# Short products on the identity added at eight places of a fixed order table

## The chip, the cores and the metric

The kernel runs on one core of one Trainium2 chip. The metric is the device time of one execution in microseconds, the median of several runs. The core has a matrix engine (TensorE, PE in the rows), a vector engine (VectorE, DVE), a scalar engine (ScalarE, ACT), a general engine (GpSimd, POOL) and a sync engine that issues transfers (SyncE, SP). They run side by side, each in the order of its own instructions, and wait for each other by semaphores. TensorE writes its results into PSUM, a small memory of eight banks.

## The reference, cut to what matters

A gated linear attention over 4 batches, 8 heads and 768 steps is followed by two feed-forward layers on 3072 rows of 384.

```python
for t in range(S):                                   # attention, D = 48
    state = alpha[:, :, t, :, None] * state + np.einsum('bhd,bhe->bhde', k[:, :, t], v[:, :, t])
    y[:, :, t] = np.einsum('bhd,bhde->bhe', q[:, :, t], state)
...
h = x @ w_in                                         # first layer, d_ff = 2048
g = (a[0] + a[1]*h + a[2]*h**2 + a[3]*h**3) / (1 + |b[0]|*|h| + |b[1]|*h**2 + 1e-6)
x = g @ w_out
...
g = x @ w_gate                                       # second layer, d_ff = 1536
out = (g * (1 / (1 + np.exp(-g))) * (x @ w_val)) @ w_out
```

## The kernel before, in words

The attention is cut into 24 blocks of 128 steps, six to a batch; blocks are numbered from 0 here. For each block TensorE transposes alpha, k and q (`aT`, `kT`, `qT`, each four transposes, line 770), makes the scores (`scores`, line 821), turns k back (`back`, `kn_ps`, line 846) and makes the update of the state and the block's output (`values`, lines 865 to 876: `upd` and `yT`). Between them VectorE scans the decays (`bb`, `cc`) and scales k and q (`kt`, line 802; `qt`, line 812), ScalarE copies results out of PSUM (`al`, `aa`, `kn`, the state `st_s`, and `yo`, line 885, the copy of `yT`), and GpSimd masks the scores and decays the state. SyncE's queue loads the blocks (`nata`, `natk`, `natq`, `natv`, line 729) and stores `yo`. The weights of both layers are loaded and split into a high and a low part (lines 639 to 702, with `win_x` and the like on VectorE, and a PSUM bank of kind `cv`). Each product of the first layer is nine matmuls of 128 x 512 (`mm1` into `h`, `mm2` into three accumulators `acc`, lines 955 to 957); the second layer follows with `pg`, `pv` and `po`. The products of the first layer begin at some 54 us, between the attention blocks.

At the start, nine transposes of the identity (`keep_warm`, line 562) run before there is data, and twenty more behind the first `qT`; they write a PSUM tile called warm.

Every piece of work is an operation of a planner, with a number in the order in which it was planned. Nothing is reordered while the kernel is built: `ORDER` is a written-out table, and each entry holds an operation's number and its way of being done:

```python
for x in table:
    i, k = x >> 1, x & 1
    ...
    yield i, how[k][2]
...
for x, (i, f) in enumerate(plan.order(ORDER)):   # i is an operation's number
```

The eight PSUM banks are given out by `order` as well. An operation that writes a bank first takes the first unit of the list `free`; the unit goes to the end of that list when the table comes to the last operation that uses it, which may be long before that operation has run on the chip. A tile with a bank's tag waits for the readers of that bank's tile before.

Eight operations have a part in the change. For each: the first unit of `free` when the table has come to it, and the operation that the table has as the last reader of that bank before.

| number | operation | what is behind it on TensorE | first free bank, its last reader by the table |
|---|---|---|---|
| 90 | `aT`, block 3 | `values`, block 1 | bank 4: ScalarE, copy of block 1's scores (45) |
| 79 | `values`, block 2 | `scores`, block 3 | bank 7: VectorE, `qt` of block 3 (99) |
| 146 | `aT`, block 5 | `values`, block 3 | no free bank |
| 135 | `values`, block 4 | `scores`, block 5 | bank 2: VectorE, `kt` of block 5 (153) |
| 161 | `values`, block 5 | `kT`, block 7 | bank 5: VectorE, `kt` of block 6 (175) |
| 185 | `values`, block 6 | `scores`, block 7 | bank 3: ScalarE, copy of block 6's scores (181) |
| 281 | `kT`, block 10 | the first `mm2` | bank 6: VectorE, `win_x`, a weight (711) |
| 942 | the first `mm2` | the second `mm2` | bank 2: ScalarE, `yo` of block 8 (241) |

Of the kernel before, what the change touches and what calls it, by code (L numbers as in the profile page):

```python
# [9 lines left out]
F32 = mybir.dt.float32  # L10
# [216 lines left out]
class Plan:  # L227
# [47 lines left out]

    def order(self, table):

        free = {c: list(range(k)) for c, k in self.classes.items()}
        todo = {}
        done = set()  # L280
        for x in table:
            i, k = x >> 1, x & 1
            _, how, deps, writes, follows = self.ops[i]
            assert i not in done and done.issuperset(deps) and done.issuperset(follows)
            done.add(i)
            for b in writes:
                if b.kind and b.ops[0] == i:
                    b.unit = free[b.cls].pop(0)
                    for j in set(b.ops):
                        todo.setdefault(j, []).append(b)  # L290
                    b.open = len(set(b.ops))
            for b in todo.get(i, ()):
                b.open -= 1
                if not b.open:
                    free[b.cls].append(b.unit)
            yield i, how[k][2]
        assert len(done) == len(self.ops)
# [160 lines left out]
def gla_moe_moe2_kernel(  # L458
# [15 lines left out]
    nc = tc.nc  # L474
# [23 lines left out]
    plan = Plan()  # L498
# [5 lines left out]
    ps = main.enter_context(tc.tile_pool(name="ps", bufs=1, space=PSUM))  # L504
# [31 lines left out]
    def fixed(t):  # L536
        b = plan.buf(None)
        b.t = t
        return b
# [10 lines left out]
    ident = const.tile([128, 128], F32, name="ident")  # L550
# [18 lines left out]
    for nm in "akqv":  # L569
        for i in range(NBV if nm == "v" else 1):  # L570
            t = A.tile([128, H, 64], F32, name=f"nat{nm}{i}")
# [164 lines left out]

    FILL = 20
    fixed_warm = fixed(warm)
    params = fixed(prm)

    def load_params():
# [590 lines left out]
    t, vs2 = end_a + 5.14, []  # L1332
# [10 lines left out]
        moe2(row, n, f0, f1, load_y(row[0], n), wg, wv, wo)  # L1343
    flag = bounds(end_a + 70.0, vs2[-1][0] - 70.0, vs2[-1][0] + 20.0)

    for x, (i, f) in enumerate(plan.order(ORDER)):
        if x == len(ORDER) - 18:
            tc.mark_branch_hint_location(
                "usual", "LikelyTaken", [mybir.EngineType.PE, mybir.EngineType.DVE, mybir.EngineType.SP])
        for b in plan.ops[i][3]:  # L1350
            if b.t is None:
                b.t = b.make()
        f()
# [40 lines left out]
```

## Time and profile before

| | us |
|---|---|
| median of 3 runs | 988.63 (988.26 to 989.31) |
| the profiled execution, its time | 987.1 |
| the profiled execution, its span from first to last instruction | 985.3 |

The trace was taken from one execution, so durations and starts are those of that one. A row of a timeline names the start in us, the length in us, the engine, the line, the operation, what is written and read, and how many alike were merged; a bracket holds the engine's idle time before it and what seems to have ended it. Matmuls overlap, so the spacing of starts tells their cost better than their lengths, and the ends of matmuls are modelled. Of a wait for several semaphores only the one that came last by the profile is named.

### The profile page before, as it was taken

The page shows a single profiled execution, that of the slowest core. Times are in us where ns is not written, and L with a number is a line of the kernel's source. Part 1 is how long each engine was busy: PE and PEld are TensorE (multiplying, and loading weights), DVE is VectorE, ACT ScalarE, POOL GpSimd, SP SyncE. Part 2 cuts the span into 40 slices and gives each one's busy share as a digit, 9 for nine tenths or more (in the row PEclk, how much of TensorE's full clock was granted, in tenths as well). Part 3 has the DMA queues.
Part 4 walks back from the last instruction along what each step waited for, and adds up shares of the span by engine and source line. Part 5 has one row for each costly group of instructions (what it writes and reads, how often), then busy time and mean ns, then how long its engine had stood idle before and what let it go on. Part 6 is the DMA issues. An engine that isn't in the chain of part 4 may idle for free.

```text
span 985.3 us, 15291 instructions
## 1 busy us (share of the span) xinstructions
PE 969.0 (98%) x5355; PEld 805.6 (82%) x5355; DVE 786.9 (80%) x1493; ACT 588.9 (60%) x1078; POOL 450.5 (46%) x426
## 2 busy tenths in 40 slices
PE   8899999999999999999999999999999999999997
PEld 7777888888888888888888888888888888888886
DVE  7999999999889888888898896799887767733222
ACT  4588998899999787789988675222122222212111
POOL 3368888799877676777987555000000000000000
PEclk9999999999999999999999999999999999999999
DMA  8978666531223242101221663346665545501000
GB/s 184 208 186 220 150 156 152 157 103 37 57 88 94 54 140 70 55 25 53 91 86 45 218 188 127 113 129 196 176 179 187 165 140 150 161 1 33 1 0 34
DMA packets 167137, 113.51 MB, mean 115 GB/s; under 512 B 115472, under 2 KB 140560, under 8 KB 167056
## 3 DMA queue, kind: packets, MB, share of 16 engines
q1 hardware_dynamic: 166768, 112.10, 40.7%
q8 instruction: 43, 0.70, 0.3%
q10 hardware_dynamic: 288, 0.39, 0.1%
q14 instruction: 38, 0.31, 0.1%
HBM read 95.95 MB, written 16.52 MB: 114 GB/s over the span
## 4 chain that ended last, share of the span: by engine, by line
PE 84%; DVE 8%; ACT 4%; issue 2%; POOL 1%; DMA 1%; SPq 0%; DVEq 0%; ACTq 0%; POOLq 0%
PE acc L955 6%; PE acc L956 6%; PE acc L957 6%; PE h L955 5%; PE h L957 5%; PE h L956 5%; PE pg L957 5%; PE pg L955 5%; PE pg L956 5%; PE pv L957 5%; PE pv L955 5%; PE pv L956 5%; PE po L955 4%; PE po L957 4%; PE po L956 4%
## 5 line engine op out<-in xcount | busy, mean ns | idle before, releaser
L925 POOL TENSOR_TENSOR gg<-t,gg 128x512 fp32r<-128x512 f32 x96 | 129.8, 1352 | 52.2 <-ACT gg L1014 50.9
L998 POOL TENSOR_TENSOR t<-t,t 128x512 f32<-128x512 f32 x96 | 127.7, 1332 | 29.2 <-ACT t L988 20.6
L1177 DVE TENSOR_TENSOR sg<-sg,pv 128x512 f32<-128x512 f32 (+1 forms) x73 | 49.4, 678 | 101.3 <-PE pv L957 101.0
L1179 ACT CAST pp<-sg 128x512 fp32r<-128x512 f32 (+1 forms) x73 | 44.8, 615 | 142.1 <-DVE sg L1177 126.7
L1175 ACT ACTIVATE sg<-pg 128x512 f32<-128x512 f32 (+1 forms) x73 | 43.0, 591 | 144.0 <-PE pg L957 143.8
L955 PE MATMUL h<-xt,win 128*128 128x512 f32 x288 | 114.4, 397 | 0.2 <-DVE wo_x L675 0.2
L955 PE MATMUL acc<-gg,wout 128*128 128x512 f32 x288 | 113.9, 396 | 0.5 <-DVE win_x L675 0.5
L957 PE MATMUL h<-xt,win 128*128 128x512 f32 x288 | 112.4, 390 | 0.0
L957 PE MATMUL acc<-gg,wout 128*128 128x512 f32 x288 | 112.3, 390 | 0.0
L956 PE MATMUL acc<-gg,wout 128*128 128x512 f32 x288 | 112.3, 390 | 0.0
L956 PE MATMUL h<-xt,win 128*128 128x512 f32 x288 | 112.2, 390 | 0.0
L957 PE MATMUL pg<-yy,wg 128*128 128x512 f32 x216 | 84.2, 390 | 0.0
L956 PE MATMUL pg<-yy,wg 128*128 128x512 f32 x216 | 84.2, 390 | 0.0
L955 PE MATMUL pg<-yy,wg 128*128 128x512 f32 x216 | 84.1, 389 | 0.0
L957 PE MATMUL pv<-yy,wv 128*128 128x512 f32 x216 | 84.0, 389 | 0.0
L956 PE MATMUL pv<-yy,wv 128*128 128x512 f32 x216 | 84.0, 389 | 0.0
L955 PE MATMUL pv<-yy,wv 128*128 128x512 f32 x216 | 84.0, 389 | 0.0
L1004 DVE SCALAR_TENSOR_TENSOR t<-t,h 128x512 f32<-128x512 f32 x96 | 65.4, 682 | 19.2 <-ACT h L1003 18.7
L995 ACT ACTIVATE t<-h,prm 128x512 f32<-128x512 f32 x96 | 73.8, 775 | 7.1 <-POOL gg L925 6.7
L1102 DVE TENSOR_SCALAR_CACHE_REDUCE chk_x<-chk_e 128x384 f32<-128x384 uint32 x136 | 73.6, 549 | 2.7
L1002 ACT ACTIVATE t<-t,oneps 128x512 f32<-128x512 f32 x96 | 69.5, 724 | 9.3 <-POOL t L998 8.9
L999 DVE TENSOR_TENSOR t<-t,h 128x512 f32<-128x512 f32 x96 | 65.1, 680 | 10.2 <-ACT t L995 10.0
(154 smaller groups left out, 2472.8 us busy)
## 6 DMA issues: line engine op xcount, KB each, us to landing
chk<-in_moe_w_out_dram SPq DMA_DIRECT2D x28, 384.0 KB, 3.2
yr<-y1d SPq DMA_DIRECT2D x36, 256.0 KB, 2.9
xr<-xd SPq DMA_DIRECT2D x27, 256.0 KB, 3.4
y1d<-ys SPq DMA_DIRECT2D x27, 256.0 KB, 3.2
win_st<-in_moe_w_in_dram SPq DMA_DIRECT2D x16, 384.0 KB, 4.1
wout_st<-in_moe_w_out_dram SPq DMA_DIRECT2D x16, 384.0 KB, 3.9
chk<-in_moe_w_in_dram SPq DMA_DIRECT2D x16, 384.0 KB, 3.5
nata<-in_alpha_dram SPq DMA_DIRECT2D x24, 192.0 KB, 3.6
```

The source lines that it names most:

```text
L925: return lambda: eng.tensor_tensor(out_(), in0(), in1().bitcast(F32), ALU.subtract)
L955: nc.tensor.matmul(out_, wh, xh, start=start, stop=False)
L956: nc.tensor.matmul(out_, wh, xl, start=False, stop=False)
L957: nc.tensor.matmul(out_, wl, xh, start=False, stop=stop)
L995: plan.op(v, [act(T, lambda: nc.scalar.activation(t4(), h(), AF.Identity, scale=a3, bias=a2), 2, False)], (hb,), (b4,))
L998: plan.op(v, [pool(T, lambda: nc.gpsimd.tensor_tensor(t1(), t1(), t2(), ALU.mult))], (b1, b2), (b1,))
L999: plan.op(v, [dve(T, lambda: nc.vector.tensor_tensor(t4(), t4(), h(), ALU.mult))], (b4, hb), (b4,))
L1002: plan.op(v, [act(T, lambda: nc.scalar.activation(t2(), t1(), AF.Ln, bias=oneps), 1)], (b1,), (b2,))
L1004: plan.op(v, [dve(T, lambda: nc.vector.scalar_tensor_tensor(t1(), t1(), ONE_EPS, h(), ALU.add, ALU.mult))], (b1, hb), (b1,))
L1102: [(DVE, 0.5, lambda: nc.vector.tensor_scalar(dst(), src(), bound, 0.0, op_, ALU.add, accum_out=cnt.t[:, c : c + 1]))],
L1177: plan.op(v, [(DVE, 0.07 + 0.53 * d, lambda sg=sg, z=z: nc.vector.tensor_tensor(sg.t[:, z], sg.t[:, z], pv.t[:, z], ALU.mult))], (sg, pv), ...
L1179: plan.op(v, [(ACT, 0.1 + 0.43 * d, lambda sg=sg, pp=pp, z=z: nc.scalar.copy(pp.t[:, 0, z], sg.t[:, z]))], (sg,), (pp,))
```

## The change

A function `fill(n)` is added. It takes the first unit of the planner's list of free banks without removing it, makes a tile in that bank and lets TensorE transpose the identity into it n times; if no bank is free, it does nothing. In the loop over the table it is called right ahead of operation i if i is a key of `fills`, when `order` has already given that operation its own banks. The table itself, and all operations in it, stay as they are. The counts add up to 39.

```diff
     def order(self, table):
 
-        free = {c: list(range(k)) for c, k in self.classes.items()}
+        free = self.free = {c: list(range(k)) for c, k in self.classes.items()}
...
+    def fill(n):
+        x = plan.free["bank"][:1]
+        if x:
+            t = ps.tile([128, 512], F32, tag=f"bank{x[0]}", bufs=1, name="fill")
+            for _ in range(n):
+                nc.tensor.transpose(t[:, 0:128], ident, ident)
...
+    fills = {
+        90: 4, 79: 5, 146: 4, 135: 10, 161: 5, 185: 5, 281: 3, 942: 3,
+    }
     for x, (i, f) in enumerate(plan.order(ORDER)):
+        if i in fills:
+            fill(fills[i])
         if x == len(ORDER) - 18:
```

## Rows read from the trace of the kernel before

**Rows 1.** Cores: span in us and mean granted TensorE clock.
```profile
core 0: 985.3 us, clock 0.998
```

**Rows 2.** Windows: length, busy us of PE, PEld, DVE, ACT, POOL; clock, DMA, GB/s.
```profile
20.00:40.00 20.00, 16.68 (x217) 14.54 (x217) 19.54 (x35) 10.96 (x27) 9.07 (x10) 1.00 0.87 192
37.00:38.00 1.00, 0.00 (x0) 0.00 (x0) 0.89 (x3) 0.93 (x3) 1.00 (x2) 1.00 0.61 182
...
40.00:80.00 40.00, 36.79 (x350) 30.73 (x350) 39.72 (x70) 32.63 (x69) 22.92 (x27) 1.00 0.83 195
80.00:200.00 120.00, 119.52 (x913) 99.57 (x911) 116.82 (x187) 108.69 (x213) 99.03 (x95) 1.00 0.65 167
200.00:979.00 779.00, 778.81 (x3708) 646.40 (x3707) 597.34 (x1188) 427.43 (x754) 313.16 (x276) 1.00 0.33 99
```

**Rows 3.** Timeline of TensorE: its eight waits of over 0.45 us by 100 us.
```profile
17.86 0.62 PE L770 MATMUL aT<-ident,nata 128*112 128x128 f32 x4 [0.63 <-DMA nata<-in_alpha_dram]
...
24.83 0.58 PE L865 MATMUL upd<-natv,kn 128*64 128x48 f32 x15 [0.87 <-ACT st_s L909]
...
30.61 0.62 PE L770 MATMUL aT<-ident,nata 128*112 128x128 f32 x4 [0.70 <-ACT wout L680]
...
38.51 0.58 PE L865 MATMUL upd<-natv,kn 128*64 128x48 f32 x15 [1.61 <-ACT kn L849]
...
44.94 1.31 PE L870 MATMUL yT<-aa,natv 128*64 128x128 f32 x16 [0.82 <-DMA natv<-in_v_dram]
...
51.03 0.58 PE L865 MATMUL upd<-natv,kn 128*64 128x48 f32 x15 [0.78 <-ACT al L779]
...
74.31 0.65 PE L770 MATMUL kT<-ident,natk 128*112 128x128 f32 x4 [0.49 <-DVE st_c L902]
75.49 0.50 PE L955 MATMUL acc<-gg,wout 128*128 128x512 f32 x1 [0.54 <-DVE win_x L675]
```

**Rows 4.** Timeline of TensorE, 6 to 9 us: products on the identity.
```profile
6.08 2.35 PE L562 MATMUL warm<-ident 128*128 128x128 f32 x20
8.26 0.60 PE L770 MATMUL aT<-ident,nata 128*112 128x128 f32 x4
```

**Rows 5.** Timeline of VectorE, 24 to 76 us: some readers of PSUM.
```profile
24.64 0.68 DVE L812 TENSOR_TENSOR qt<-qT,bb 112x512 f32<-112x512 f32 x1
...
30.43 0.68 DVE L802 TENSOR_TENSOR kt<-kT,cc 112x512 f32<-112x512 f32 x1
...
39.38 0.69 DVE L802 TENSOR_TENSOR kt<-kT,cc 112x512 f32<-112x512 f32 x1
...
43.91 0.68 DVE L802 TENSOR_TENSOR kt<-kT,cc 112x512 f32<-112x512 f32 x1
...
50.43 0.68 DVE L812 TENSOR_TENSOR qt<-qT,bb 112x512 f32<-112x512 f32 x1
...
74.91 0.53 DVE L675 SCALAR_TENSOR_TENSOR win_x<-win_st,win_e 128x384 uint32<-128x384 uint32 x1
```

**Rows 6.** Timeline of ScalarE, 28 to 78 us: copies of scores, state and output.
```profile
28.63 0.58 ACT L830 COPY aa<-sc 128x512 f32<-128x512 f32 x1 [3.04 <-PE sc L821]
...
30.93 0.35 ACT L909 COPY st_s<-st_c 48x192 f32<-48x192 f32 x1
...
76.87 0.62 ACT L885 COPY yo<-yT 128x512 f32<-128x512 f32 x1
```

**Rows 7.** Timeline of TensorE, 28 to 50 us: some transposes and one `values`.
```profile
28.87 0.60 PE L770 MATMUL kT<-ident,natk 128*112 128x128 f32 x4
...
31.38 0.58 PE L865 MATMUL upd<-natv,kn 128*64 128x48 f32 x15
...
42.11 0.65 PE L770 MATMUL kT<-ident,natk 128*112 128x128 f32 x4
...
49.21 0.60 PE L770 MATMUL qT<-ident,natq 128*112 128x128 f32 x4
```

**Rows 8.** Timeline of TensorE: its last wait of over 0.2 us.
```profile
141.00 0.61 PE L865 MATMUL upd<-natv,kn 128*64 128x48 f32 x15 [0.41 <-DVE t L1010]
```

## Prediction

> **What bounds the kernel now.** I read the cores first, for the span and the clock, then windows by stage, then TensorE's waits in its timeline, and last VectorE and ScalarE around them. The profiled execution took 987.1 us, 985.3 of them span [rows 1]. The reader is to see two stages. From 200 to 979 us TensorE is busy in 778.81 of 779 us, from 80 to 200 in 119.52 of 120 [rows 2]: what it loses before then comes out at the end. From 20 to 80 us VectorE is busy in 19.54 of 20 and 39.72 of 40 us, and TensorE waits [rows 2, 3]: there VectorE sets the pace, and a delay of VectorE is not made good. The eight waits of the title are all in this part, 6.44 us together [rows 3].
>
> The granted clock is 1.00, the 2.4 GHz level, in each of these windows, also from 37 to 38 us, which holds no matmul at all [rows 2]. There is no slow stretch for the fills to lift.
>
> **What the change adds.** Nothing is removed or moved. The keys are the numbers of the operations that wait, so each fill stands on TensorE right ahead of its wait's operation. The price of a product: twenty begin at 6.08 us, the next transposes at 8.26, so 2.18/20 = 0.109 us [rows 4]. The counts are indeed 0.7 of each wait: 10 x 0.109 = 1.09 of 1.61. At operation 146 the list of free banks is empty, so no fill is made: 35 products, 3.8 us, remain. Were all hidden, they would cost nothing.
>
> But a fill needs a bank, and `free` follows the table, not the chip. A bank stands in it as soon as the table has passed its last reader, and on the chip that reader, on VectorE or ScalarE, may still be waiting for its turn. The fill must wait for it, and the operation behind the fill waits too, though its own bank and data are ready. That is the step on which the time hangs. I take the fills in order.
>
> - Operation 90 (block 3, 4 products, 0.44 us in a wait of 0.63 for a load): the bank was read by ScalarE's copies of block 1's scores, which TensorE has outrun by a full block. Hidden; at most 0.44.
> - Operation 79 (block 2, 5 products): the bank's last reader is VectorE's qt of block 3, 24.64 + 0.68 = 25.32 [rows 5]. `values` itself began at 24.83 [rows 3]. With 0.05 for the signal (as from 75.44, the end of win_x, to the product at 75.49 [rows 3, 5]) and 5 x 0.109, `values` starts at 25.92: 1.09 late. Who waits? The scores of block 3 are behind it on TensorE, ScalarE sat idle 3.04 us for them, and its state copy of block 3, which ends at 30.93 + 0.35 and releases `values` at 31.38 [rows 6, 7], stands behind: 1.1 late again. The load that holds operation 146 takes up part for the transposes alone. On VectorE, kt of block 4 needs transposes that now end at 28.87 + 0.60 + 1.09 = 30.56 [rows 7], and goes from 30.43 to 30.61 [rows 5]: all of VectorE is 0.2 late.
> - Operation 135 (block 4, 10 products): the last reader is kt of block 5, 39.38 + 0.69 + 0.2 = 40.27 [rows 5]. `values` would have begun at 38.51, or some 0.3 later by now [rows 3]. The fill starts at 40.32 and lasts 1.09: `values` at 41.41, 2.9 late. The scores of block 5 and the k transposes behind them move with it, from 42.11 to 45.01, and end at 45.66 [rows 7]; kt of block 6 on VectorE goes from 43.91 to 45.71 [rows 5], 1.8 late.
> - Operation 161 (block 5, 5 products): the bank is read by that kt, until 45.71 + 0.68 = 46.39. Behind the transposes this costs TensorE little; `values` waits for the masks of its late scores anyway. Carry 2.9, less 0.4 if the load named in its row was the last to come [rows 3].
> - Operation 185 (block 6, 5 products, 0.55 in a wait of 0.78): the bank is read by ScalarE's copies of the scores, which are ahead of the masks that `values` needs. Hidden; at most 0.55. TensorE goes on 2.9 late. VectorE's qt at 50.43 needs transposes that end at 49.21 + 0.60 + 2.9 = 52.71 [rows 7]: it starts at 52.76, so VectorE is 2.3 late, and as it is full, so it stays up to 75 us.
> - Operation 281 (block 10, 3 products): the last reader is VectorE's win_x, 74.91 + 0.53 = 75.44 [rows 5], while the transposes began at 74.31 [rows 3]. In the old times: fill at 75.49, out at 75.82, 1.51 late. That win_x also frees the next operation's accumulator, so this alone would matter little.
> - Operation 942 (the first product into the accumulators, 3 products): the last reader is ScalarE's yo of block 8, 76.87 + 0.62 = 77.49 [rows 6], which this product had no need of. Fill at 77.54, product at 77.87 instead of 75.49: 2.38 late. On top of VectorE's 2.3 (ScalarE works off VectorE's results here, so I move yo by the same): 4.7 late at 75 us.
>
> From here TensorE is full and keeps the 4.7. What takes up some of it is the one wait left by 200 us, 0.41 at 141.00 [rows 8]: VectorE and ScalarE are less late than TensorE now, so it goes. The sum: 2.3 + 2.38 - 0.4 = 4.3 us. Profiled execution: 987.1 to 991.4. The median of the runs shown lies 1.5 us above that execution, and on it I forecast 988.63 + 4.3 = **992.9 us**.
>
> Bounds of the uncertain terms: the carry up to 75 us from 0 (if all of it is taken up) to 2.9 (if ScalarE moves with TensorE and not with VectorE); I take 2.3, the row that is nearest. The two fills at 75 us: 2.38, or 2.05 if the three products ran beside other work. The wait at 141: 0 to 0.41 taken up.
>
> Does a waiting fill hold what is behind it? From 37 to 38 us there is no matmul in the window while `values` waits, though the next block's transposes stand behind it [rows 2, 3]. With that the two fills at 75 us cost 2.38; if the transposes and products could pass, they would cost 0. The Trainium skill ("TensorE: Matmul & The Clock Gate", Part 3, "What overlaps and what doesn't") says that matmuls start and end strictly in program order and only weight loads are pulled ahead, which speaks against fills that have a wait of their own. The trace agrees, with no matmul in that microsecond.
>
> **The rivals.**
> - Only the end of the early part counts. VectorE's delay of 2.3 us is made good before 75 us, in pauses that the rows don't show, and 2.38 - 0.4 = 2.0 is left: 990.6 us. For it: TensorE has 6.4 us of waits. Against it: VectorE has 0.74 us of pauses between 20 and 80 us.
> - Hidden, as the title has it: each fill finds a bank that is long read, since the first unit of the list is the one that the table freed first. Then the end moves by nothing: 988.6 us, no change. It decides where the readers end before the wait's end less the fill: 24.28 for operation 79, 37.42 for 135, 73.98 for 281, 75.16 for 942. For it: 90 and 185 are like that. Against it: the other four readers end at 25.32, 40.07, 75.44 and 77.49 [rows 5, 6].
> - Faster, by the clock: if matmuls behind the waits ran at the lower level, the fills would give back up to half of their time. Sixteen updates behind 1.61 us of waiting have the same 0.58 as those behind none [rows 3, 7], so there is nothing to give back: 988.6 at best, and below it only if the runs differ. The Trainium skill (same page, Part 1) has it that idleness brings the throttle and activity lifts it, and by that rule fills in waits are of use. The trace's 1.00 in an idle window says not here.
> - More than forecast: carry 2.9, nothing given back at 141, and some tenths behind it in the first layer: 5.3 to 6, 994 to 994.6 us.
>
> **How the numbers follow.** Forecast 0.74; only the end counts 0.10; hidden 0.08; more 0.05; faster 0.03. A difference under 0.2%, 2.0 us, is about what a measurement of this kernel can't tell from none. The second case lies on that border, so it is halved: slower 0.74 + 0.05 + 0.06 = 0.85, same 0.08 + 0.04 = 0.12, faster 0.03. Range: from 990.4 (only the end counts) to 994.6 (more), which leaves out the hidden and the faster case.
>
> **What would show it.** In the profile after: tiles named fill on TensorE, 31 to 35 products; a wait for VectorE's qt ahead of a fill near 25.3 us and for its kt near 40.3; `values` of block 4 at about 41.4 and not 38.51; the fill near 80 us waiting for ScalarE's yo; the first product into `acc` at about 80.2 instead of 75.49; then the same spacing to the end. The prediction is wrong if the fills start with the waits, if VectorE's win_x is less than 1.5 us later than 74.91, or if the distance between the kernels shrinks behind 80 us by more than 0.5.

## The result, and the profile after

| | us |
|---|---|
| before, median of 4 runs on the same chip | 988.72 (988.26 to 989.31) |
| after, median of 4 runs | 998.41 (998.23 to 1000.74) |
| ratio, with its 95% interval | 1.0103 [1.0086, 1.0121] |
| the profiled execution after, its time | 998.33 |

The changed kernel is slower, as forecast, but by 9.7 us and not by 4.3, and outside the range of 990.4 to 994.6. In the rows below the lines of the old code are 7 higher than before (`upd` is line 872, `kt` 809, `qt` 819), and the products of the fills are line 745.

The cores of the kernel after, beside [rows 1]:

```profile
core 0: 996.6 us, clock 0.994
```

Windows of the kernel after (length, busy us of PE, PEld, DVE, ACT, POOL; granted clock, DMA, GB/s), beside [rows 2]; the last three are shorter:

```profile
20.00:40.00 20.00, 16.73 (x186) 14.57 (x186) 18.10 (x29) 8.72 (x21) 6.05 (x9) 0.91 0.72 156
40.00:80.00 40.00, 35.70 (x355) 30.07 (x354) 35.59 (x61) 26.80 (x58) 19.61 (x22) 0.96 0.74 175
80.00:200.00 120.00, 117.46 (x892) 97.74 (x890) 114.95 (x184) 106.30 (x209) 95.02 (x91) 0.99 0.65 167
200.00:985.00 785.00, 784.83 (x3757) 650.93 (x3757) 605.31 (x1198) 437.30 (x771) 322.81 (x285) 1.00 0.34 100
26.50:29.50 3.00, 2.97 (x30) 2.64 (x32) 2.97 (x7) 0.00 (x0) 0.00 (x0) 0.50 0.44 130
43.00:46.00 3.00, 2.90 (x26) 2.60 (x26) 1.28 (x2) 0.00 (x0) 0.00 (x0) 0.54 0.91 192
84.00:86.00 2.00, 1.46 (x8) 1.05 (x9) 2.00 (x3) 2.00 (x5) 0.92 (x2) 0.54 1.12 217
```

Two things differ from [rows 2]. VectorE, which was full from 40 to 80 us (39.72 of 40), is now busy for 35.59: it waits as well. And the granted clock, 1.00 throughout [rows 2], is 0.50 from 26.5 to 29.5 us, 0.54 from 43 to 46 and 0.54 from 84 to 86, so at its 1.2 GHz level for most of these stretches. From 200 us on all is as it was.

The timeline of TensorE in the kernel after, its waits and what follows them, beside [rows 3] and [rows 8]:

```profile
26.53 1.33 PE L745 MATMUL fill<-ident 128*128 128x128 f32 x5 [2.95 <-DVE qt L819]
27.79 0.98 PE L872 MATMUL upd<-natv,kn 128*64 128x48 f32 x15
...
43.10 2.28 PE L745 MATMUL fill<-ident 128*128 128x128 f32 x10 [2.79 <-DVE kt L809]
45.31 0.98 PE L872 MATMUL upd<-natv,kn 128*64 128x48 f32 x15
...
57.72 0.73 PE L745 MATMUL fill<-ident 128*128 128x128 f32 x5
...
83.87 0.66 PE L745 MATMUL fill<-ident 128*128 128x128 f32 x3 [1.64 <-DVE win_x L675]
84.32 1.06 PE L777 MATMUL kT<-ident,natk 128*112 128x128 f32 x4
85.92 0.90 PE L745 MATMUL fill<-ident 128*128 128x128 f32 x3 [0.54 <-ACT yo L892]
86.47 0.78 PE L962 MATMUL acc<-gg,wout 128*128 128x512 f32 x1
...
152.18 0.61 PE L872 MATMUL upd<-natv,kn 128*64 128x48 f32 x15 [0.37 <-DVE t L1017]
```

The four fills that were said to wait do wait, for the four readers named: `qt`, `kt`, `win_x`, `yo`. The fill at 57.72, which was said to be hidden, has no wait. But behind the two longest waits the products come at twice their price: the ten at 43.10 are followed by `upd` 2.21 us later, 0.22 each and not 0.109 [rows 4], and `upd` takes 0.98 where it took 0.58 [rows 3]. The first product into `acc` begins at 86.47, 10.98 later than at 75.49 [rows 3], and `upd` with the old wait of 0.41 at 152.18, 11.18 later than at 141.00 [rows 8]: its wait is still there.

VectorE and, in the second fence, ScalarE in the kernel after, beside [rows 5] and [rows 6]:

```profile
22.34 2.74 DVE L801 TENSOR_TENSOR_SCAN cc<-al,seed_r 112x516 f32<-112x516 f32 x1
...
25.80 0.68 DVE L819 TENSOR_TENSOR qt<-qT,bb 112x512 f32<-112x512 f32 x1
...
33.33 0.69 DVE L809 TENSOR_TENSOR kt<-kT,cc 112x512 f32<-112x512 f32 x1 [1.59 <-PE kT L777]
...
42.27 0.68 DVE L809 TENSOR_TENSOR kt<-kT,cc 112x512 f32<-112x512 f32 x1
...
46.53 0.36 DVE L909 TENSOR_TENSOR st_c<-upd,st_c 112x192 f32<-112x192 f32 x1 [2.22 <-PE upd L872]
...
83.29 0.52 DVE L675 SCALAR_TENSOR_TENSOR win_x<-win_st,win_e 128x384 uint32<-128x384 uint32 x1
...
91.85 0.69 DVE L819 TENSOR_TENSOR qt<-qT,bb 112x512 f32<-112x512 f32 x1 [2.60 <-PE qT L777]
```
```profile
85.24 0.62 ACT L892 COPY yo<-yT 128x512 f32<-128x512 f32 x1
```

So `qt` of block 3 ends at 26.48 and not at 25.32, because the scan ahead of it took 2.74 us. The kernel before does that too, as its second trace shows (below). VectorE now waits 1.59 and 2.22 us for TensorE, where the forecast had it 0.2 late at the first place.

### The profile page after: what moved, and what is told of

The parts are those of the page before. It is cut to its first block, busy times and chain, and to the rows that moved or that the text cites. A ratio compares the mean times of both kernels' runs of the same rounds, so it can differ in the third digit from the quotient of the medians.

```text
span 996.6 us, 15365 instructions
## 1 busy us (share of the span) xinstructions
PE 978.0 (98%) x5390; PEld 813.3 (82%) x5390; DVE 789.8 (79%) x1493; ACT 589.6 (59%) x1078; POOL 449.8 (45%) x426
## 4 chain that ended last, share of the span: by engine, by line
PE 84%; DVE 8%; ACT 4%; issue 2%; POOL 1%; DMA 1%; SPq 0%; DVEq 0%; ACTq 0%; POOLq 0%
PE acc L962 6%; PE acc L963 6%; PE acc L964 6%; PE h L962 5%; PE h L964 5%; PE h L963 5%; PE pg L963 5%; PE pg L964 5%; PE pg L962 5%; PE pv L963 5%; PE pv L964 5%; PE pv L962 5%; PE po L963 4%; PE po L964 4%; PE po L962 4%
```

## The experiments

The theory after the result: the waits for banks cost about what was forecast, and the clock that falls behind them costs the rest. The rivals: the products themselves cost it; or the late masks and scores behind `values` cost it, whatever the clock.

The eleven runs were made on three chips (1 to 4, 5 to 8, and 9 to 11); each ratio is to runs of the kernel before on the same chip. Single executions differ by several us here (the kernel before from 987.18 to 997.67 over these chips), so ratios carry the sizes, and traces the places.

**1. The same fills in banks that are already read; none at 281 and 942.** The tile is taken from a later place in the list.

```diff
+    def fill(n, k):
+        x = plan.free["bank"][k : k + 1]
...
+    90: (4, 0), 79: (5, 1), 135: (10, 1), 161: (5, 3), 185: (5, 0),
```

> The first five fills that were made (operations 90, 79, 135, 161 and 185; 29 products), each in a bank of the free list that its reader has long left, and none for 281 and 942, where no such bank is in the list. Theory A (a fill costs by the wait for its bank's reader, and by what that wait does to the clock; the products themselves are hidden in the waits): as the kernel before, 988.7 us within 0.7, the waits shortened to about 0.3 of what they were, the granted clock 1.00 from 20 to 80 us. Theory B (35 products on TensorE cost their own time wherever they stand): 29 x 0.109 = 3.2 us more, 991.9 us.

Measured: 0.9995 [0.9979, 1.0010]. Its timeline of TensorE:

```profile
23.71 0.71 PE L745 MATMUL fill<-ident 128*128 128x128 f32 x5
26.00 0.58 PE L872 MATMUL upd<-natv,kn 128*64 128x48 f32 x15 [1.58 <-ACT al L786]
...
38.36 1.25 PE L745 MATMUL fill<-ident 128*128 128x128 f32 x10
39.67 0.58 PE L872 MATMUL upd<-natv,kn 128*64 128x48 f32 x15
...
76.53 0.50 PE L962 MATMUL acc<-gg,wout 128*128 128x512 f32 x1 [0.54 <-DVE win_x L675]
```

The products start at once. Where they wait for no bank, they cost nothing that these runs can tell: 29 products at 0.109 would be 3.2 us, and the interval leaves 1.0 at most. What costs is which bank they take.

**2 to 4. One part alone:** only operation 79 in the second kernel; only 135 in the third; only 281 and 942 in the fourth.

```diff
-    90: 4, 79: 5, 146: 4, 135: 10, 161: 5, 185: 5, 281: 3, 942: 3,
+    79: 5,
```
```diff
+    135: 10,
```
```diff
+    281: 3, 942: 3,
```

> Only the fill of operation 79, in its bank of the changed kernel. Theory A without the clock (the step of the prediction): the fill waits for VectorE's qt to about 25.4 us, the block is 1.1 us late, VectorE 0.2 us, and the end moves by 0.2 us: 988.9 us. Theory A with the clock: TensorE stands idle for 1.5 us or, if VectorE's scan before that qt is 2.7 us long as in the changed kernel, for 2.9 us; in the second case the granted clock falls to 0.5 behind it, the block is 2.7 us or more late, VectorE as well, and the end moves by 2 to 3 us: 991.3 us.

> Only the fill of operation 135 (10 products, its bank read by VectorE's kt that ends at 40.07 us in the kernel before). Without the clock: values of block 4 at 41.2 us, 2.65 late, VectorE 1.5 late, 990.2 us. With the clock: TensorE is idle from 36.9 to 40.2 us, the granted clock is about 0.5 behind that, the ten products take 2.2 us and not 1.1, values is about 4.5 late, and the end moves by 3.5 to 4.5: 992.7 us.

> Only the two fills near 75 us, in their banks of the changed kernel. Without the clock: the first product into acc at 77.9 and not 75.5, 0.4 of it given back at 141 us: 988.7 + 2.0 = 990.7 us. With the clock: the two waits, 1.6 and 0.5 us, with little between them, bring the granted clock to about 0.5 for 2 to 3 us, as in the changed kernel from 84 to 88 us, which adds 1 to 1.7: 992.0 us.

Measured: 0.9990 [0.9962, 1.0017], 1.0046 [1.0029, 1.0063] and 1.0013 [0.9989, 1.0038]. Of single parts only 135 is told from no change. Its 0.46% (4.6 us) is near the 3.5 to 4.5 expected with the clock, but that is luck in part: experiment 5 keeps the clock and costs almost the same. Its timeline of TensorE has the wait, and its window from 44 to 46 us has the clock at 0.50:

```profile
42.12 1.28 PE L745 MATMUL fill<-ident 128*128 128x128 f32 x10 [3.30 <-DVE kt L809]
43.34 0.93 PE L872 MATMUL upd<-natv,kn 128*64 128x48 f32 x15
```
```profile
42.00:44.00 2.00, 1.88 (x26) 1.74 (x27) 1.29 (x2) 0.00 (x0) 0.00 (x0) 0.86 0.84 171
44.00:46.00 2.00, 2.00 (x23) 1.70 (x19) 1.51 (x4) 0.00 (x0) 0.68 (x1) 0.50 0.89 221
```

The three together are +0.49%, the whole change +1.03%. In the profiled spans (990.1, 993.4 and 990.0 against 986.9 of the kernel before in experiment 8) they add up to 12.8, more than the 9.7 (first trace) or 11.7 (experiment 7) of the whole. So whether the parts add isn't settled by these runs.

**5. Operation 135 alone, with TensorE kept busy through its wait:** 26 products in a bank that is read, then the ten that wait.

```diff
+    135: ((26, 1), (10, 0)),
...
+            for count, at in fills[i]:
+                fill(count, at)
```

> The kernel with only the fill of operation 135 (995.1 us, beside 990.1 for the kernel before), and ahead of that fill 26 more products in the second bank of the list, which has long been read; they fill the 2.8 us in which TensorE stood idle. The wait for VectorE's kt and the ten products behind it stay. If the idle time lowers the clock and that is a large part of the loss: granted clock 1.00 from 42 to 47 us, the ten products in 1.1 us, values and the block's output 1.2 us shorter, the end 2 to 3 us earlier than 995.1, about 992.5. If the loss is the wait for the bank alone: unchanged, 995 us, or later.

Measured: 1.0042 [1.0028, 1.0056]. The clock is 1.00 in every window from 20 to 90 us, and the first product into `acc` begins at 81.07 instead of 82.88 in experiment 3; but the ratios of the two don't differ (0.04 points, give or take 0.22). So by the ratios at least about half of what 135 costs by itself is the wait for its bank and not the clock, and the middle values say nearly all. VectorE shows why it's more than the 2.3 us of the forecast. Its `qt` of block 7 is 2.53 late (54.88 against 52.35 in experiment 8), near the forecast; its `qt` at 75.81 is 3.53 late (against 72.28). Two shifts nearly cancel in these: this execution is 0.5 late before its fill (the scan `cc` of block 3 at 22.90, against 22.42), and experiment 8 has a fall of the clock of its own (below). Against experiment 1, which has no fall, and with the starts set equal, the first is 2.8 (51.58 and 22.37 there). Between the two, VectorE in experiment 5 loses 1.0 us: 0.44 in one scan that is stretched from 1.22, 0.11 in another, and 0.42 in two new waits for ScalarE:

```profile
56.41 1.66 DVE L793 TENSOR_TENSOR_SCAN bb<-al,seed_f 112x516 f32<-112x516 f32 x1
...
63.21 0.69 DVE L1006 TENSOR_TENSOR t<-t,h 128x512 f32<-128x512 f32 x1 [0.23 <-ACT t L991]
...
76.69 0.69 DVE L1006 TENSOR_TENSOR t<-t,h 128x512 f32<-128x512 f32 x1 [0.19 <-ACT t L1002]
```

**6. The change with one product in each fill.**

```diff
+    90: 1, 79: 1, 146: 1, 135: 1, 161: 1, 185: 1, 281: 1, 942: 1,
```

> All fills in the banks of the changed kernel, each with one product only: 7 products instead of 35. If the waits for the banks and the clock behind them make the loss: 1.4 to 2.9 us are saved on the products that stood behind the waits (18 of them at 0.11 to 0.22 us), and the most is left: 994 to 997 us, with waits of about 3 us for qt and for kt still there. If the products make the loss: within 1 us of the kernel before.

Measured: 1.0085 [1.0058, 1.0113], beside 1.0102 [1.0077, 1.0128] for the change on the same chip. Its fills wait 2.19, 3.29, 1.30 and 1.27 us. 28 products fewer give back 0.17% by the ratios, and the intervals overlap, so this run alone doesn't bound the products closely. With experiments 1 and 10, where 29 products cost nothing that the runs can tell and the change with 50 products more costs less than the change, they are at most a small part.

**7 and 8. The change, and the kernel before, traced again** (no edit).

> The changed kernel as it is, on the same chip as the others, for the comparison: about 998.4 us, with VectorE's scan before qt 2.7 us long. If that long scan comes only by chance, this run shows it at 1.6 us and is about 1 to 2 us faster.

> The kernel before as it is. The trace read for the prediction had VectorE's scan of block 3 at 1.57 us; in all five other traces, four of them without a fill ahead of that scan or with a hidden one, it was 2.73. If the long scan is a state that the kernel before has as well: 2.7 us here, a wait of about 2 us ahead of values of block 2, and the granted clock below 1 behind it, with 989 to 991 us. If the fills bring it: 1.6 us.

Measured: 1.0102 [1.0077, 1.0128] and 0.9998 [0.9970, 1.0026]. The second trace of the kernel before, 986.9 us long, differs from the one that the forecast rests on. VectorE, TensorE, and a window of it:

```profile
22.42 2.73 DVE L794 TENSOR_TENSOR_SCAN cc<-al,seed_r 112x516 f32<-112x516 f32 x1
```
```profile
26.05 0.71 PE L865 MATMUL upd<-natv,kn 128*64 128x48 f32 x15 [2.48 <-ACT al L779]
...
77.30 0.50 PE L955 MATMUL acc<-gg,wout 128*128 128x512 f32 x1 [0.54 <-DVE win_x L675]
...
142.75 0.61 PE L865 MATMUL upd<-natv,kn 128*64 128x48 f32 x15 [0.36 <-DVE t L1010]
```
```profile
20.00:40.00 20.00, 16.35 (x182) 14.36 (x180) 18.96 (x31) 9.72 (x24) 7.03 (x10) 0.91 0.74 169
```

The scan takes 2.73 us, TensorE waits 2.48 for its result, and the clock falls, without any fill. The 1.57 us of the first trace was the exception: all twelve other traces have 2.73 or 2.74.

**9 and 10. The change without 135, and the change whole, but kept busy through the waits at 79 and 135.**

```diff
-    90: 4, 79: 5, 146: 4, 135: 10, 161: 5, 185: 5, 281: 3, 942: 3,
+    90: 4, 79: 5, 146: 4, 161: 5, 185: 5, 281: 3, 942: 3,
```
```diff
+    90: ((4, 0),), 79: ((24, 1), (5, 0)), 135: ((26, 1), (10, 0)),
+    161: ((5, 0),), 185: ((5, 0),), 281: ((3, 0),), 942: ((3, 0),),
```

> The change without the fill at operation 135 (the others as in the change). Theory A, the costs add: only 79 gave +0.6 us, only 281 and 942 gave +1.5, so this gives +2 (about 991.6 where the kernel before stands at 989.5), first product into acc some 2 us later than in the kernel before. Theory B, the costs of the early fills lift each other (three parts alone add up to +7.1, the whole is +9.7 to +10.2), and it is 79 together with 281 and 942 that does it: +4.5 to +5, about 994.3. If A holds, the surplus of about 3 us belongs to 135 in company with 79.

> The change with its waits for banks as they are, but with 24 products at 79 and 26 at 135 in a bank that is already read, ahead of the fill that waits, so that TensorE isn't idle there. Theory A, the lower clock behind the waits at 79 and 135 is a main part of what the forecast lacked (about 3 to 3.5 us of granted clock are lost there in the change): about 3 us below the change, +6.5 to +7 over the kernel before, clock 1.00 from 23 to 60 us. Theory B, what counts is when masks, scores and states behind the waits come, and VectorE would have been late anyway: 1 us or less below the change, +9 or more, with the clock at 1.00 all the same.

Measured: 1.0028 [1.0012, 1.0044] and 1.0053 [1.0035, 1.0071]. By the ninth, 135 in company is worth 0.74 points of the whole 1.02, more than the 0.46 that it costs alone; this favours the reading that its cost grows beside the others, though the intervals are wide. The tenth answers the main question. It has the same fills in the same banks, and 50 products more. By the ratios it costs half as much as the change (by the medians 6.3 us against 10.2), and its interval lies below that of the change, 1.0077 to 1.0128, which was measured on another chip. TensorE and windows of the tenth:

```profile
23.46 2.78 PE L745 MATMUL fill<-ident 128*128 128x128 f32 x24
26.57 0.76 PE L745 MATMUL fill<-ident 128*128 128x128 f32 x5 [0.33 <-DVE qt L819]
27.27 0.61 PE L872 MATMUL upd<-natv,kn 128*64 128x48 f32 x15
...
39.47 4.09 PE L745 MATMUL fill<-ident 128*128 128x128 f32 x36
43.49 0.61 PE L872 MATMUL upd<-natv,kn 128*64 128x48 f32 x15
...
83.84 0.78 PE L962 MATMUL acc<-gg,wout 128*128 128x512 f32 x1
```
```profile
26.00:30.00 4.00, 3.67 (x50) 2.96 (x50) 3.96 (x9) 0.04 (x1) 0.51 (x1) 1.00 0.57 143
...
42.00:46.00 4.00, 4.00 (x55) 3.56 (x53) 2.66 (x6) 0.00 (x0) 0.68 (x1) 1.00 1.05 235
```

VectorE of the tenth:

```profile
40.93 0.68 DVE L809 TENSOR_TENSOR kt<-kT,cc 112x512 f32<-112x512 f32 x1
...
80.86 0.53 DVE L675 SCALAR_TENSOR_TENSOR win_x<-win_st,win_e 128x384 uint32<-128x384 uint32 x1
```

Where the clock stayed at 1.00, `upd` takes 0.61 and not 0.98. At 79 the bank comes no earlier (`qt` ends at 26.52, against 26.48 in the kernel after), but what is behind it runs at its old speed, and `kt` of block 4 begins at 31.98 and not at 33.33. So the bank of 135 comes 1.3 sooner: `kt` of block 5 ends at 41.61 and not at 42.95. A fall of the clock at 79 thus makes the wait at 135 longer, which is one way in which the parts lift each other. The 26 products outlast that bank: from 39.47 on at 0.11 each they end at 42.4, an estimate. So the tenth keeps the fills and the clock, but not every wait as it was.

**11. The first experiment with 16 products at 79.**

```diff
-    90: (4, 0), 79: (5, 1), 135: (10, 1), 161: (5, 3), 185: (5, 0),
+    90: (4, 0), 79: (16, 1), 135: (10, 1), 161: (5, 3), 185: (5, 0),
```

> The fills of operations 90, 79, 135, 161 and 185 in banks that are already read, none at 281 and 942, and 16 products at 79 in place of 5. With 5 the granted clock was already 1.00 behind a wait of 1.58 us. Theory A, nothing is left to win there: the same as with 5, 0.5 to 1 us below the kernel before, ratio about 0.9993, not told apart from 1. Theory B, with 5 products the clock falls in part of the executions and with 16 it doesn't: 1.5 us below, ratio about 0.9985.

Measured: 1.0022 [1.0001, 1.0042], neither of the two: if anything a little slower than the kernel before. Its profiled execution (988.5 us) looks like that of the first experiment, but its twelve runs spread from 988.5 to 996.26, and the longer ones have the lower mean clock (988.5 us at 0.999, 996.26 at 0.996). Where the longer ones lost it isn't in any trace that I have. So no version here is shown to beat the kernel before; the first experiment isn't told from it.

## Why the prediction missed

**What held.** The mechanism: `free` follows the table, so a fill waits for its bank's last reader, and what stands behind it on TensorE waits too. The four readers named are the four in the trace, the fills at 161 and 185 have no wait of their own (in experiment 9 the one at 161 does: 1.02 us, for `kt`), operation 146 makes no fill (35 products). Experiment 1 shows it from the other side: 29 of the same products in other banks cost nothing that its runs can tell. The first rival (only the end counts, 990.6) fell: the early part counts most. "Hidden" holds only with the banks changed.

**What failed**, summed on three profiled executions that reach the scan `cc` of block 3 at the same time (22.34 to 22.42 us): the change (its first trace, span 996.6 us), the change kept busy (10, span 994.9) and the kernel before (8, span 986.9), whose first products into `acc` begin at 86.47, 83.84 and 77.30. Experiment 7 is left out of the sum, since it is 0.9 late already at its first fill (17.94, against 17.05 in the first trace). The change is 9.7 us longer than the kernel before. The forecast had 4.7 at 75 us, less 0.4.

| step of the prediction | forecast | runs | missing |
|---|---|---|---|
| delay up to the first product into `acc`, change kept busy | 4.7 | 83.84 - 77.30 = 6.54 | 1.84 |
| lower clock up to there ("no slow stretch") | 0 | 86.47 - 83.84 = 2.63 | 2.63 |
| behind it: span less that start, 910.13 against 909.6 | 0 | 0.53 | 0.53 |
| wait at 141 us taken up | -0.4 | 0 | 0.4 |

4.3 + 1.84 + 2.63 + 0.53 + 0.4 = 9.7. What the granted clock lacks of 1.00, summed over windows of 1 us from 20 to 100 us, is 5.1 us in the kernel after (three falls), 1.7 in the tenth (one fall, at 84 us), 1.7 in experiment 8 (one, near 27 us), and nothing in experiments 1, 5 and 11. The change thus lost 3.4 us more of clock than the kernel before, about what the second and third rows add up to. The split between the first two rows isn't exact, since the fall in experiment 8 moves its own first product: experiment 1, without a fall, has it at 76.53, 0.8 sooner. By the ratios the change costs 1.02% (10 us) and the tenth 0.53% (5.2 us, from 3.5 to 7.0), so with most of the clock kept the forecast of 4.3 is within its interval. That doesn't confirm its terms: the traces of the tenth and of experiment 8 are 8.0 apart, and the first row is 1.84 over.

- The step that failed worst is the one on the clock: "there is no slow stretch for the fills to lift", and with it the price of 0.109 us for every product and 0.58 for `upd`. I read it from windows with a clock of 1.00, one of them without a matmul, and from `upd` behind a wait of 1.61 us. Neither excluded a fall behind a longer wait, and the change made longer ones: 2.95, 2.79 and 1.64 us, each with products or transposes at the lower level behind it (the four `kT` at 84.32, for instance, take 1.06 us, for 0.60 to 0.65 in [rows 7]). The doubled price stood in the trace before, ahead of the rows that the forecast used: its first four `aT` take 1.07 us, and the four at 8.26 us 0.60 [rows 4].

```profile
3.79 1.07 PE L770 MATMUL aT<-ident,nata 128*112 128x128 f32 x4 [0.18 <-DMA nata<-in_alpha_dram]
```

  An idle window's own 1.00 says nothing of what comes next. In experiment 7 there is no matmul from 26 to 27 us, at 1.00; the work resumes at 27.42, and the fall shows from 28 to 31; in the first trace after, at the same wait, it came before the work resumed at 26.53 (0.88 from 26.0 to 26.2 us, 0.50 from 26.2 to 26.5):

```profile
26.00:27.00 1.00, 0.00 (x0) 0.00 (x0) 0.92 (x2) 0.78 (x2) 0.00 (x0) 1.00 0.96 182
27.00:28.00 1.00, 0.58 (x5) 0.53 (x5) 1.00 (x3) 0.00 (x0) 0.00 (x0) 1.00 0.82 165
28.00:29.00 1.00, 1.00 (x21) 0.88 (x21) 1.00 (x3) 0.00 (x0) 0.00 (x0) 0.69 0.10 22
29.00:31.00 2.00, 2.00 (x18) 1.67 (x15) 1.97 (x5) 0.00 (x0) 0.66 (x1) 0.50 0.64 207
```

  The Trainium skill ("TensorE: Matmul & The Clock Gate", Part 1) has idleness bring the throttle and activity lift it. I set it aside for gains and never asked what new idle time would do by it; the trace after agrees with it (0.50 from 26.5 to 29.5 us, at the end of the wait of 2.95).
- Operation 135: "`values` at 41.41, 2.9 late" came out at 45.31 in the trace after, which has 79's delay and the low clock in it. By itself (experiment 5) its carry was 2.5 to 2.8 us at the `qt` that the forecast named, for 2.3. "As it is full, so it stays up to 75 us" was wrong: it grew by 1.0, in scans that took longer, with GpSimd's shifted work beside them, and in waits for ScalarE. In the tenth VectorE is 4.1 late at `win_x` (80.86, against 76.72 in experiment 8), for 2.3, and the two fills at 75 us add 2.4 to that, for 2.38. So the 1.84 of the first row is VectorE's carry, and the term of the two fills was right.
- Operation 79: "VectorE is 0.2 late" rested on a scan of 1.57 us. In the usual 2.73 `qt` ends 1.2 later, the wait grows to 1.87 (experiment 2) or as much as 2.95 us (the kernel after), and the clock falls by its end. By itself this cost nothing that its runs can tell (0.9990 [0.9962, 1.0017]). That fits experiment 8, where the kernel before waits 2.48 us there for `al`, with a fall of the clock of its own.
- Operations 281 and 942: 2.38 forecast, 0.13% (1.3 us, from -1.1 to 3.8) alone. Behind them the clock falls in experiments 4, 6, 7, 9 and 10 too; in the first trace after a part of that fall lies ahead of the first product into `acc`, in the second row, and the rest in the third.
- The wait at 141 us: TensorE's delay should have taken it up. It stays, 0.36 in experiment 8 and 0.37 in the kernel after: what it waits for, a result of VectorE, is late by the same amount. VectorE was 6.6 late at `win_x` (83.29, against 76.72), but its `qt` at 91.85 waits 2.60 us for TensorE and is 9.3 late (82.59 in experiment 8): from there VectorE has TensorE's delay.
- Two slips in the forecast's numbers change nothing of this: the chance of 0.10 is split 0.06 to 0.04 and not halved, and the lower end, 990.4, should be the 990.6 of its case.

## What to carry to other kernels

Filler work must not be able to wait: give it a unit whose last reader has ended on the chip, by the trace, and not one that a list calls free. When a change lengthens an idle stretch of TensorE, price what follows it at the lower clock too, and keep that end in the range. A trace of one execution is one draw: a duration on which a step rests is worth a second trace.

## What I had not expected of the hardware

- The length of the last wait alone doesn't tell whether the clock falls. It fell at the end of waits of 2.95, 2.48 and 1.69 us or just behind them (after, experiment 8, experiment 4 at 25.97), and not behind 1.90 (experiment 5 at 26.53, 1.00 in each window from 20 to 90) nor 1.61 [rows 3]. What decides between them stays open.
- Twenty-four and thirty-six fp32 transposes of the identity in a row, with nothing else, ran at 0.11 us each and left the clock at 1.00 (experiment 10).
- A scan of 112 x 516 took 1.22, 1.57, 1.66 or 2.74 us. In each of these longer ones GpSimd was at work beside it. In the first trace before GpSimd's two selects took 2.13 us and the scan 1.57; in the trace after the selects took 1.22 and the scan 2.74. That the two slow each other fits these rows, but no run here separates it.

```profile
22.82 2.13 POOL L835 TENSOR_SCALAR_AFFINE_SELECT aa<-aa 128x512 f32<-128x512 f32 x2
```
```profile
22.78 1.22 POOL L842 TENSOR_SCALAR_AFFINE_SELECT aa<-aa 128x512 f32<-128x512 f32 x2
```
